# State products of the fourth and fifth chunk moved ahead of the layer products in a decay-attention and gated-MLP kernel

## Chip, cores and metric

One core of a Trainium2 chip runs the whole program in one launch. The metric is the device time of that core in microseconds: the median of three runs.

## What is computed

Decay attention over 2 batches, 8 heads, 768 positions and 64 columns a head, then two gated layers over the 1536 tokens of width 512. The attention part is computed in blocks, with a state of 64x64 per head that is carried from block to block:

```python
intra = np.einsum('bhic,bhjc->bhij', qb, kb) * Dmask[None]
intra = np.einsum('bhij,bhjd->bhid', intra, vb)
inter = np.einsum('bhid,bhde->bhie', qb * lam_pow[None], kv_state)
out[:, :, sl] = intra + inter
kb_dec = kb * rev_pow[None]
kv_state = lam_block[None, :, None, None] * kv_state + np.einsum('bhsd,bhse->bhde', kb_dec, vb)
...
a = x @ w_a
b = x @ w_b
return (a * b @ w_out).astype(np.float32)
...
h = np.maximum(np.maximum(x @ w1, x @ w2), x @ w3)
return (h @ w_out).astype(np.float32)
```

## The kernel before

The kernel takes the 768 positions in 6 chunks of 128, and each chunk for both batches at once (`pair(m)` gives the two indices n of chunk m, counted from 0, so the fourth and fifth chunk are m = 3 and m = 4). For a chunk TensorE does four kinds of small products: `scores(n)` (queries with keys, in 64x64 pieces of the array, closed by two small matmuls on zeros per quarter, L508), `earlier(n)` (queries with the state, 64x64, L575; called state products below), `within(n)` (masked scores with values, 128x64, L588; called masked products) and `update(n)` (keys with values, 128x64, L601).

Other engines work in between. `masked(n)` on VectorE multiplies the scores with the decay table (L521, two banks for each n, four instructions a chunk). `queries(n)` and `keys(n)` on GpSimd scale queries and keys (L548, L553). `carry(m)` on VectorE folds the update into the state `held`, which lies in the tile `stt`, in four quarters of two heads (L617). `taken(n)` on ScalarE copies the results out of PSUM.

Into these chunks the first layer is mixed. `layer1` is a generator: each `next(layer1)` puts one step of 12 matmuls of 384 columns into TensorE's stream (`plain_group`, L753), in which weights and inputs stand as a high and a low part, so that there are three products for each. After the chunks, the layers go on in a scheme with seven products of sums of blocks, which need sums such as S1, S2, S3 and S4 of the inputs (tile `x0s` for the first three chunks, `x1s` for the others) and T1 to T4 of the weights (tile `wd` for weight 1, `w` for weight 2). Each operand is split in two: a copy on ScalarE gives the high part (`hi`, `x0S`), a subtraction on VectorE or GpSimd the low part (`lo`, `x0S` again).

These sums and splits are tasks of a planner, `Pace`. It runs while the program is written, keeps an estimated time for each engine, and puts a task's next instruction into the program as soon as the engine is free by its estimate. An instruction marked `EITHER` goes to VectorE or GpSimd, whichever would end first by the estimate. A task stops at a `gate` until `pace.open` names it. So a change in the order of TensorE's work changes also which engine gets which sum and in which order. Within one engine the order is then fixed: each engine works through its own stream and waits at its head.

Of the kernel before, what the change touches and what calls it, by code (L numbers as in the profile page):

```python
# [169 lines left out]
def decay_attention_gated_mlps(ctx: ExitStack, tc: tile.TileContext, qkv: bass.AP, lam: bass.AP, wup: bass.AP, wdown: bass.AP, out: bass.AP):  # L170
# [7 lines left out]
    pace = Pace()  # L178

    def slot(name, dt=F32):  # L180
        return sp.tile([128, 1536], dt, tag="s", name=name)
# [7 lines left out]
    def rd(t):  # L189
        return t.bitcast(F32)  # L190

    def tt(e, o, a, b, op):
        (nc.vector if e == "DVE" else nc.gpsimd).tensor_tensor(out=o, in0=a, in1=b, op=op)  # L193

    def copy(o, a):
        nc.scalar.activation(out=o, in_=a, func=AF.Copy)  # L196
# [44 lines left out]
    def converted(m, width, roomy=False):  # L241

        load_to(m)
        double = raw.pop(m)[:, 0:width]
        yield ("ACT",), width + 60, "S"
        if width > WB:
            near = wp.tile([128, width], F32, tag="s", bufs=1, name=f"ws{m}")
            scaled(double, near)  # L250
            yield ("ACT",), width + 60, "S"
        t = slot(f"wd{m}") if roomy else hp.tile([128, 1792], F32, tag="h", name=f"w{m}")
        w = t[:, 0:width]
        below(double, w)
        if width == WB:
            near = t[:, WB:2 * WB]
            yield ("ACT",), width + 60, "S"
            scaled(double, near)
        if m not in BYDVE:
            yield ("ACT",), width + 330, "S"  # L260
            sign(double, w)
        if m > 1:
            load_to(m + 2)
        yield ("DVE",), width, "S"
        joined(near, w)
        if m in BYDVE:
            yield ("DVE",), width, "S"
            signed(near, w)
        return t
# [36 lines left out]
    def up_pair(m, i):  # L306

        o = wop[m] = {}
        if m > 0:
            yield "gate", ("done", m - 1)  # L310
        yield "gate", ("conv", m)
        plain = i < NPLAIN
        t = yield from converted(m, 1024, plain)
        if not plain:
            yield from block_sums(t)
        yield "gate", ("split", m)
        hi, lo = (slot(f"{x}{m}", F32R) if plain else hp.tile([128, 1792], F32R, tag="h", name=f"{x}{m}") for x in ("hi", "lo"))
        for s in (slice(0, 1024), slice(1024, 1792))[0:1 if plain else 2]:
            n = s.stop - s.start
            yield ("ACT",), n, "S"  # L320
            copy(hi[:, s], t[:, s])
            e = yield EITHER, n, "S"
            tt(e, lo[:, s], t[:, s], rd(hi[:, s]), ALU.subtract)
            for x, place in PLACE.items():
                if s.start <= place.start < s.stop:
                    o["B12" if plain and x == "T2" else x] = (hi[:, place], lo[:, place])
        pace.open(("done", m))
        if plain:
            yield "gate", ("late", m)
            last = slot(f"hl{m}", F32R)  # L330
            t6 = t.rearrange("p (a n) -> p a n", a=6)
            e = yield EITHER, 512, "S"
            tt(e, t6[:, 4:6], t6[:, 0:1].to_broadcast([128, 2, 256]), t6[:, 1:4:2], ALU.subtract)
            e = yield EITHER, 256, "S"
            tt(e, t6[:, 0], t6[:, 3], t6[:, 4], ALU.subtract)
            e = yield EITHER, 256, "S"
            tt(e, t6[:, 1], t6[:, 2], t6[:, 0], ALU.subtract)
            for s, names in ((slice(1024, 1536), ("T1", "T3")), (slice(256, 512), ("T4",)), (slice(0, 256), ("T2",))):
                n = s.stop - s.start
                h, l = (last[:, x:x + 256] for x in (0, 256)) if names[0] == "T4" else (hi[:, s], lo[:, s])  # L340
                yield ("ACT",), n, "S"
                copy(h, t[:, s])
                e = yield EITHER, n, "S"
                tt(e, l, t[:, s], rd(h), ALU.subtract)
                for k, x in enumerate(names):
                    o[x] = h[:, 256 * k:256 * k + 256], l[:, 256 * k:256 * k + 256]

    def block_sums(t):

        t7 = t.rearrange("p (a n) -> p a n", a=7)  # L350
        e = yield EITHER, 512, "S"
        tt(e, t7[:, 4:6], t7[:, 0:1].to_broadcast([128, 2, 256]), t7[:, 1:4:2], ALU.subtract)
        e = yield EITHER, 256, "S"
        tt(e, t7[:, 0], t7[:, 3], t7[:, 4], ALU.subtract)
        e = yield EITHER, 256, "S"
        tt(e, t7[:, 6], t7[:, 2], t7[:, 0], ALU.subtract)
# [47 lines left out]
    def open_to(what, m):  # L404
        if m < len(items):
            items_to(m)
            pace.open((what, m))
# [53 lines left out]
    def rows(i):  # L461
        return slice(64 * i, 64 * i + 64)

    def pair(m):
        return 2 * m, 2 * m + 1
# [90 lines left out]
    def place(n, h):  # L556
        w = h // 2 % 2
        banks, o = ob[n]
        return banks[h // 4][rows(h % 2), o + 128 * w:o + 128 * w + 128]
# [8 lines left out]
    def earlier(n):  # L568

        q = aq[n][:, 1024:1536]  # L570
        for w in range(2):
            for i in range(2):
                for x in range(2):
                    a = 2 * w + x
                    nc.tensor.matmul(  # L575
                        place(n, 4 * i + a), held[rows(i), n % 2, a], q[rows(i), 128 * a:128 * a + 128],
                        start=ob[n][1] == 0 and w == 0, stop=False, skip_group_check=True)
        pace.pe(0.5, max(at["qs", n], at["st"]))
# [401 lines left out]
    with tc.manual_schedule():  # L980
# [71 lines left out]
        def layer1_steps():  # L1052
            for i, j in ((0, 0), (1, 0), (0, 1)):
                if j == 0:
                    ga[i] = slot(f"g{i}")
                yield from plain_group(i, j)
                if (i, j) == (NPLAIN - 1, 0):
                    pace.open(("x0", "S3"))
                    pace.open(("x1", "sums"))
                if j == 1:  # L1060
                    finished1(0, Group("", i, j, None, None))
                    open_to("split", NPLAIN + 1)
            groups = [Group(f"u{i}_{j}", i, j, xo.get, gated) for i, j in plan]
            for i, _ in enumerate(in_slots(groups, each1, finished1)):
                if 7 * len(groups) - i == 3:
                    next(then)
                elif 7 * len(groups) - i == 5:
                    pace.need(gtasks[0, 0][0])
                yield
# [13 lines left out]
        yo = {}  # L1083
        then = down1(at1)
        layer1 = layer1_steps()

        def steps(task, n, e=None):
# [105 lines left out]
        for m in range(3, NC):  # L1193
            last = m == NC - 1
            if m == 4:
                load_to(NPLAIN)
                for i in range(2):
                    for n in pair(5):
                        load(n, i)
                load_to(NPLAIN + 1)  # L1200
                open_to("conv", NPLAIN)
                pace.open(("late", 1))
                open_to("split", NPLAIN)
            for n in pair(m):
                queries(n)
            if not last:
                for n in pair(m):
                    keys(n)
            for n in pair(m):
                scores(n)  # L1210
                masked(n)
            for _ in range(1 if last else 2):
                next(layer1)
            results(m, last)
            for n in pair(m):
                earlier(n)
            for n in pair(m):
                within(n)
            if last:
                for n in pair(m):  # L1220
                    for i in range(2):
                        taken(n, xa, part=i)
                        if n % 2 == i == 0:
                            operands(1)
                        x = f"A{n % 2 + 1}{i + 1}"
                        pace.open(("x1", x))
                        steps(xo[1].tasks[x], 2)
            else:
                for n in pair(m):
                    taken(n, xa)  # L1230
            if m == 3:
                pace.open(("x0", "sums"))
            if not last:
                for n in pair(m):
                    update(n)
                carry(m)
            else:
                next(layer1)
# [175 lines left out]
```

## Time and profile before

| | us |
|---|---|
| median of 3 runs | 500.21 (499.57 to 500.47) |
| profiled execution | 499.4 |
| its span, first to last instruction | 497.6 |
| TensorE busy (matmuls) | 493.3 (99%) |
| VectorE busy | 343.5 (69%) |
| ScalarE busy | 295.5 (59%) |
| GpSimd busy | 60.3 (12%) |

Busy times are of one profiled execution; the span lies 1.8 us under that execution's own time. The page calls TensorE's matmuls PE, VectorE DVE, ScalarE ACT and GpSimd POOL. A timeline row gives the start from the beginning of the span, the duration from the first start to the last end of the merged instructions, the engine, the line, what is written and read, the shape and the count. Square brackets name the idle time ahead of it and what ended it. Matmuls are pipelined, so rows on PE overlap by some tenths of a microsecond, and the distance between starts is what counts. Rows on the other engines overlap by 0.07 to 0.1.

### The profile page before, as it was taken

To read this page: it belongs to the slowest core of one execution; us is meant where nothing else is said; L and a number is where in the kernel's file an instruction comes from. 1 tells how busy PE (TensorE), PEld (TensorE's weight loads), DVE (VectorE), ACT (ScalarE), POOL (GpSimd) and SP (SyncE) were. 2 spreads that over 40 slices of the span, in tenths; PEclk is the share of its full clock that TensorE was granted. 3 is DMA by queue.
4 is the path that set the end of the run, shared out by engine and by line. 5 is a ranking of instruction groups with operands and counts; after the bars stand their busy time and mean duration, and the time that the engine had idled before them with its cause. 6 is when DMAs were issued, how large, how long until landed. Compare 5 with 4: busy or idle time off the path is not lost.

```text
span 497.6 us, 8202 instructions
## 1 busy us (share of the span) xinstructions
PE 493.3 (99%) x3351; PEld 465.3 (94%) x3351; DVE 343.5 (69%) x536; ACT 295.5 (59%) x464; POOL 60.3 (12%) x58
## 2 busy tenths in 40 slices
PE   9999999999999999999999999999999999999997
PEld 6999999999999999998888888999999999998897
DVE  6779886667657656577364189667867885787962
ACT  3867675654465654679572566545666455576561
POOL 4885201101111110120000000000000000000000
PEclk9999999999999999999999999999999999999999
DMA  8996002222222101315231022002202211120023
GB/s 301 414 413 231 1 0 86 84 86 86 86 86 85 60 8 61 126 65 189 87 95 76 0 84 86 0 1 85 86 1 84 86 63 65 63 65 0 22 107 126
DMA packets 10597, 46.66 MB, mean 94 GB/s; under 512 B 1216, under 2 KB 1472, under 8 KB 8000
## 3 DMA queue, kind: packets, MB, share of 16 engines
q1 hardware_dynamic: 10512, 46.14, 25.2%
q8 instruction: 26, 0.43, 0.4%
q14 instruction: 11, 0.09, 0.1%
q10 hardware_dynamic: 48, 0.00, 0.0%
HBM read 42.99 MB, written 3.15 MB: 93 GB/s over the span
## 4 chain that ended last, share of the span: by engine, by line
PE 99%; POOL 0%; ACT 0%; DVE 0%; issue 0%; POOLq 0%
PE yp L851 20%; PE zu L731 18%; PE zv L731 15%; PE bu L731 9%; PE bv L731 8%; PE p L753 5%; PE out L905 5%; PE xu L731 4%; PE xv L731 4%; PE zo L954 3%; PE o L588 2%; PE bo L954 1%; PE s L496 1%; PE o L575 1%; PE k L601 1%; PE s L503 1%
## 5 line engine op out<-in xcount | busy, mean ns | idle before, releaser
L193 DVE TENSOR_TENSOR lo<-w,hi 128x1024 fp32r<-128x1024 f32 (+2 forms) x39 | 42.5, 1091 | 11.6 <-ACT hi L196 11.4
L196 ACT ACTIVATE hi<-w 128x1024 fp32r<-128x1024 f32 (+2 forms) x40 | 37.4, 935 | 11.5 <-DVE w L193 4.9
L851 PE MATMUL yp<-gh,dh 128*128 128x512 f32 x108 | 42.0, 389 | 0.0
L851 PE MATMUL yp<-gl,dh 128*128 128x512 f32 x108 | 42.0, 389 | 0.0
L851 PE MATMUL yp<-gh,dl 128*128 128x512 f32 x108 | 42.0, 389 | 0.0
L783 POOL TENSOR_TENSOR g<-z1u,z6u 128x384 f32<-128x384 f32 x21 | 22.6, 1076 | 147.6 <-DVE z6u L765 147.6
L193 DVE TENSOR_TENSOR gl<-g,gh 128x512 fp32r<-128x512 f32 x36 | 25.2, 719 | 20.7 <-ACT gh L196 20.7
L239 DVE SCALAR_TENSOR_TENSOR w<-ws,w 128x1024 int32<-128x1024 int32 (+1 forms) x21 | 30.4, 1445 | 8.9 <-ACT w L228 6.8
L228 ACT ACTIVATE w<-wr 128x1024 f16<-128x1024 f32 (+2 forms) x26 | 33.1, 1273 | 0.2
L193 DVE TENSOR_TENSOR w<-w 128x256 f32<-128x256 f32 (+1 forms) x57 | 30.6, 538 | 1.3
L223 ACT ACTIVATE w<-wr 128x1024 int32<-128x1024 uint16 (+2 forms) x26 | 27.5, 1057 | 2.4 <-DVE lo L193 2.0
L765 DVE TENSOR_TENSOR z6u<-bu,z6u 128x384 f32<-128x384 f32 x21 | 11.7, 555 | 23.7 <-PE bu L731 23.7
L196 ACT ACTIVATE z6u<-zu 128x384 f32<-128x384 f32 x21 | 10.2, 486 | 27.4 <-PE zu L731 27.4
L196 ACT ACTIVATE gh<-g 128x512 fp32r<-128x512 f32 x36 | 21.4, 622 | 7.5 <-PE yp L851 7.5
L231 ACT ACTIVATE ws<-wr 128x1024 f32<-128x1024 f32 (+1 forms) x22 | 24.2, 1098 | 0.8 <-DMA wr<-wup_dram 0.8
L196 ACT ACTIVATE z7u<-zu 128x384 f32<-128x384 f32 x21 | 10.3, 492 | 23.5 <-PE zu L731 23.4
L851 PEld LDWEIGHTS yp<-gh,dh 128*128 128x128 f32 x108 | 20.3, 188 | 4.2
L851 PEld LDWEIGHTS yp<-gl,dh 128*128 128x128 f32 x108 | 20.3, 188 | 4.2
L851 PEld LDWEIGHTS yp<-gh,dl 128*128 128x128 f32 x108 | 20.3, 188 | 4.1
L731 PE MATMUL bu<-x1S,hi 128*128 128x384 f32 x88 | 22.3, 334 | 0.0
L731 PE MATMUL zu<-x1S,hi 128*128 128x384 f32 x88 | 22.3, 334 | 0.0
L731 PE MATMUL zu<-x1A,hi 128*128 128x384 f32 x84 | 21.3, 334 | 0.0
(260 smaller groups left out, 1448.2 us busy)
## 6 DMA issues: line engine op xcount, KB each, us to landing
wr<-wup_dram SPq DMA_DIRECT2D x20, 1024.0 KB, 4.7
wr<-wdown_dram SPq DMA_DIRECT2D x12, 768.0 KB, 4.3
aq<-qkv_dram SPq DMA_DIRECT2D x12, 512.0 KB, 7.8
av<-qkv_dram SPq DMA_DIRECT2D x6, 512.0 KB, 9.0
out_dram<-ob SPq DMA_DIRECT2D x11, 256.0 KB, 2.0
av<-qkv_dram SPq DMA_DIRECT2D x8, 256.0 KB, 8.3
wr<-wup_dram SPq DMA_DIRECT2D x2, 512.0 KB, 8.9
out_dram<-ob SPq DMA_DIRECT2D x2, 128.0 KB, 1.8
```

The lines of the kernel that those rows point to most:

```text
L193: (nc.vector if e == "DVE" else nc.gpsimd).tensor_tensor(out=o, in0=a, in1=b, op=op)
L196: nc.scalar.activation(out=o, in_=a, func=AF.Copy)
L223: nc.scalar.activation(out=w.bitcast(I32), in_=halves[:, :, 1], func=AF.Copy, scale=2.0 ** -13, bias=2.0 ** -14 - 0.5)
L228: nc.scalar.activation(out=o[:, :, 1], in_=high(double), func=AF.Copy, scale=2.0 ** -112)
L231: nc.scalar.activation(out=near, in_=high(double), func=AF.Copy, scale=2.0 ** -112)
L239: nc.vector.scalar_tensor_tensor(out=w, in0=near, scalar=3, in1=w, op0=ALU.logical_shift_left, op1=ALU.bitwise_or)
L731: nc.tensor.matmul(ps, w, x, start=p in FIRST and i == 0, stop=i == len(todo) - 1, skip_group_check=p not in FIRST)
L753: nc.tensor.matmul(ps, w, x, start=m == 0, stop=m == 11)
L783: nc.gpsimd.tensor_tensor(out=ga[g.n][:, tokens(g.j, 0)], in0=g.z[1], in1=g.z[6], op=ALU.mult)
L851: nc.tensor.matmul(ps[e], w[:, cols], g, start=k == 0 and m == 0, stop=k == K1 - 1 and m == 2)
L905: nc.tensor.matmul(ps, a[:, o:o + 128], w[:, s], start=k == 0 and n == 0, stop=k == K2 - 1 and n == 2)
L954: nc.tensor.matmul(ps, x[:, 128 * r:128 * r + 128], w, start=p in FIRST and n == 0, stop=n == 8, skip_group_check=p not in FIRST)
```

## The change

In the fourth and fifth chunk the two layer steps stood between scores and state products. They now stand between state products and masked products. The sixth chunk keeps its order. Besides, the last split of weight 1 (its block T2) gets a gate of its own, which opens with the second plain group of the first layer. The diff:

```diff
@@ -337,6 +337,8 @@
             tt(e, t6[:, 1], t6[:, 2], t6[:, 0], ALU.subtract)
             for s, names in ((slice(1024, 1536), ("T1", "T3")), (slice(256, 512), ("T4",)), (slice(0, 256), ("T2",))):
                 n = s.stop - s.start
+                if names[0] == "T2":
+                    yield "gate", ("plain", m)
                 h, l = (last[:, x:x + 256] for x in (0, 256)) if names[0] == "T4" else (hi[:, s], lo[:, s])
                 yield ("ACT",), n, "S"
                 copy(h, t[:, s])
@@ -1055,6 +1057,7 @@
                     ga[i] = slot(f"g{i}")
                 yield from plain_group(i, j)
                 if (i, j) == (NPLAIN - 1, 0):
+                    pace.open(("plain", i))
                     pace.open(("x0", "S3"))
                     pace.open(("x1", "sums"))
                 if j == 1:
@@ -1209,11 +1212,14 @@
             for n in pair(m):
                 scores(n)
                 masked(n)
-            for _ in range(1 if last else 2):
+            if last:
                 next(layer1)
             results(m, last)
             for n in pair(m):
                 earlier(n)
+            if not last:
+                for _ in range(2):
+                    next(layer1)
             for n in pair(m):
                 within(n)
             if last:
```

TensorE in the fifth chunk before, from the last matmul of its scores (p is a bank of layer products, o a bank of the attention's results, am the masked scores):

```order
L508 MATMUL s_1_697<-stt 64x2x64
L753 MATMUL p_726<-xh_201,hi_584 128x384
...
L753 MATMUL p_745<-xl_202,hi_584 128x384
L575 MATMUL o_0_764<-aq_426,stt 64x128 x2
...
L588 MATMUL o_0_764<-am_693,av_430 64x128 x2
```

The same place now:

```order
L510 MATMUL s_1_699<-stt 64x2x64
L577 MATMUL o_0_726<-aq_426,stt 64x128 x2
...
L755 MATMUL p_752<-xh_201,hi_588 128x384
...
L755 MATMUL p_775<-xl_202,hi_588 128x384
L590 MATMUL o_0_726<-am_695,av_430 64x128 x2
```

The 16 state products, which read `stt`, now follow the scores at once; the 24 layer products stand behind them. The fourth chunk reads the same.

VectorE from the split of weight 1 in the fourth chunk to the first mask of the fifth, before (g is the gated product of the first layer):

```order
L760 TENSOR_TENSOR g_445<-p_569,z_474 128x384
L193 TENSOR_TENSOR lo_585<-wd_566,hi_584 128x1024
L193 TENSOR_TENSOR x0s_444<-x_207 128x768
L617 SCALAR_TENSOR_TENSOR stt<-stt,tables,k_629 128x2x64 x4
L521 TENSOR_TENSOR am_693<-s_0_669,tables 128x512
```

and now:

```order
L762 TENSOR_TENSOR g_445<-p_573,z_459 128x384
L193 TENSOR_TENSOR lo_589<-wd_571,hi_588 128x1024
L762 TENSOR_TENSOR g_445<-p_591,z_474 128x384
L193 TENSOR_TENSOR x0s_444<-x_207 128x768
L193 TENSOR_TENSOR x0s_444<-x0s_444,x_200 128x768
L619 SCALAR_TENSOR_TENSOR stt<-stt,tables,k_629 128x2x64 x4
L523 TENSOR_TENSOR am_695<-s_0_671,tables 128x512
```

One of the two gating products and the sum S2 (`x0s` from `x0s` and `x`) now stand between the split and the state.

GpSimd from the scaled keys of the fifth chunk on, before:

```order
L553 TENSOR_TENSOR av_432<-av_432,tables 128x512
L193 TENSOR_TENSOR x0s_444<-x0s_444,x_200 128x768
L193 TENSOR_TENSOR wd_566<-wd_566 128x512
L548 TENSOR_TENSOR aq_654<-aq_654,tables 128x512
L548 TENSOR_TENSOR aq_656<-aq_656,tables 128x512
L193 TENSOR_TENSOR lo_784<-w_718,hi_783 128x768
L193 TENSOR_TENSOR x0s_444<-x_200,x0s_444 128x768
```

and now:

```order
L555 TENSOR_TENSOR av_432<-av_432,tables 128x512
L193 TENSOR_TENSOR wd_571<-wd_571 128x512
L193 TENSOR_TENSOR wd_571<-wd_571 128x256 x2
L550 TENSOR_TENSOR aq_656<-aq_656,tables 128x512
L550 TENSOR_TENSOR aq_658<-aq_658,tables 128x512
L193 TENSOR_TENSOR lo_589<-wd_571,hi_588 128x512
```

GpSimd gave the sums S2 and S4 and a split of 768 columns of weight 2 to VectorE, and took two sums of 256 and a split of 512 of weight 1 from it.

VectorE in the fifth chunk, from the join of weight 2 (L239) to the state, before:

```order
L239 SCALAR_TENSOR_TENSOR w_718<-ws_691,w_718 128x1024
L193 TENSOR_TENSOR w_718<-w_718 128x512
L193 TENSOR_TENSOR w_718<-w_718 128x256
L760 TENSOR_TENSOR g_725<-p_745,z_743 128x384
...
L193 TENSOR_TENSOR x0S_639<-x0s_444,x0S_639 128x768
L193 TENSOR_TENSOR lo_784<-w_718,hi_783 128x1024
L193 TENSOR_TENSOR x0S_721<-x0s_444,x0S_721 128x768
L617 SCALAR_TENSOR_TENSOR stt<-stt,tables,k_808 128x2x64 x4
```

and now:

```order
L239 SCALAR_TENSOR_TENSOR w_720<-ws_693,w_720 128x1024
L193 TENSOR_TENSOR w_720<-w_720 128x512
L193 TENSOR_TENSOR w_720<-w_720 128x256 x2
L193 TENSOR_TENSOR x0S_639<-x0s_444,x0S_639 128x768
L193 TENSOR_TENSOR lo_769<-w_720,hi_768 128x1024
L762 TENSOR_TENSOR g_751<-p_775,z_773 128x384
L193 TENSOR_TENSOR x0S_649<-x0s_444,x0S_649 128x768
L193 TENSOR_TENSOR lo_769<-w_720,hi_768 128x768
L193 TENSOR_TENSOR x0s_444<-x_200,x0s_444 128x768
L619 SCALAR_TENSOR_TENSOR stt<-stt,tables,k_813 128x2x64 x4
```

A split of 768 and the sum S4 joined the row ahead of the state that the sixth chunk reads.

## Rows read from the trace of the kernel before

**Rows 1.** The page, busy time, share of the span and instructions by engine.
```profile
PE 493.3 (99%) x3351; PEld 465.3 (94%) x3351; DVE 343.5 (69%) x536; ACT 295.5 (59%) x464; POOL 60.3 (12%) x58
```

**Rows 2.** Busy times by stretch; PEclk is TensorE's granted clock.
```profile
core 0: us, PE busy (x) PEld busy (x) DVE busy (x) ACT busy (x) POOL busy (x), PEclk, DMA share, GB/s
27.80:64.82 37.02, 37.02 (x596) 35.13 (x593) 33.56 (x52) 23.81 (x39) 18.04 (x12) 1.00 0.47 184
64.82:490.00 425.18, 425.18 (x2333) 403.76 (x2333) 288.92 (x441) 254.40 (x382) 22.59 (x21) 1.00 0.19 66
```

**Rows 3.** TensorE's timeline, fourth to sixth chunk: start, duration, instruction.
```profile
29.41 0.44 PE L753 MATMUL p<-xh,hi 128*128 128x384 f32 x1
...
33.51 0.34 PE L753 MATMUL p<-xl,hi 128*128 128x384 f32 x1
33.78 1.10 PE L575 MATMUL o<-aq,stt 64*64 64x128 f32 x32
34.81 1.97 PE L588 MATMUL o<-am,av 128*64 128x128 f32 x32
36.61 1.10 PE L601 MATMUL k<-av 128*64 128x64 f32 x32
...
39.25 0.44 PE L753 MATMUL p<-xh,hi 128*128 128x384 f32 x1
...
49.09 0.44 PE L753 MATMUL p<-xh,hi 128*128 128x384 f32 x1
...
51.38 1.10 PE L575 MATMUL o<-aq,stt 64*64 64x128 f32 x32
```

**Rows 4.** VectorE's timeline in the same chunks.
```profile
27.92 1.12 DVE L617 SCALAR_TENSOR_TENSOR stt<-stt,tables,k 128x128 f32<-128x128 f32 x4 [0.28 <-PE k L601]
...
35.43 1.78 DVE L193 TENSOR_TENSOR lo<-wd,hi 128x1024 fp32r<-128x1024 f32 x1 [0.76 <-POOL av L553]
37.14 0.94 DVE L193 TENSOR_TENSOR x0s<-x 128x768 f32<-128x768 f32 x1
38.01 1.11 DVE L617 SCALAR_TENSOR_TENSOR stt<-stt,tables,k 128x128 f32<-128x128 f32 x4
...
41.44 2.26 DVE L239 SCALAR_TENSOR_TENSOR w<-ws,w 128x1024 int32<-128x1024 int32 x1
43.73 1.65 DVE L193 TENSOR_TENSOR w<-w 128x512 f32<-128x512 f32 x1
45.41 0.42 DVE L193 TENSOR_TENSOR w<-w 128x256 f32<-128x256 f32 x1
45.75 0.55 DVE L760 TENSOR_TENSOR g<-p,z 128x384 f32<-128x384 f32 x1
...
47.42 1.22 DVE L193 TENSOR_TENSOR lo<-w,hi 128x1024 fp32r<-128x1024 f32 x1
...
50.46 2.47 DVE L521 TENSOR_TENSOR am<-s,tables 128x512 f32<-128x512 f32 x4
```

**Rows 5.** GpSimd's timeline in the same chunks.
```profile
24.10 2.99 POOL L548 TENSOR_TENSOR aq<-aq,tables 128x512 f32<-128x512 f32 x2
...
33.06 3.07 POOL L553 TENSOR_TENSOR av<-av,tables 128x512 f32<-128x512 f32 x2
38.25 1.85 POOL L193 TENSOR_TENSOR x0s<-x0s,x 128x768 f32<-128x768 f32 x1 [2.12 <-DVE x0s L193]
40.05 1.32 POOL L193 TENSOR_TENSOR wd<-wd 128x512 f32<-128x512 f32 x1
41.31 3.52 POOL L548 TENSOR_TENSOR aq<-aq,tables 128x512 f32<-128x512 f32 x2
```

**Rows 6.** ScalarE's timeline in the fifth chunk.
```profile
39.98 1.40 ACT L228 ACTIVATE w<-wr 128x1024 f16<-128x1024 f32 x1
...
42.05 0.85 ACT L196 ACTIVATE x0S<-x0s 128x768 fp32r<-128x768 f32 x1
...
45.93 1.06 ACT L196 ACTIVATE hi<-w 128x1024 fp32r<-128x1024 f32 x1 [0.69 <-DVE w L193]
```

## Prediction

> **What bounds the kernel now.** I read the page first. TensorE is busy for 493.3 us, 99% of the span [rows 1]. The busy times by stretch then show where the rest lies: from 27.80 to 490 us TensorE is busy in all of both stretches, at a granted clock of 1.00 [rows 2]. So the end is set by TensorE's own instruction stream: what lengthens or shortens that stream, or makes it wait, moves the end by the same amount, and no later slack gives it back. The question is then only what the change does to TensorE's stream and which waits it puts into it. For this I read TensorE's timeline from the fourth to the sixth chunk [rows 3], where one stage follows another with no gap, and the timelines of the engines that feed it: VectorE [rows 4], GpSimd [rows 5] and ScalarE [rows 6].
>
> The fourth chunk's stream is: scores, then from 29.41 two steps of layer products (24 matmuls, 4.37 us), from 33.78 the state products, from 34.81 the masked products, from 36.61 update and scores of the fifth chunk, whose layer products start at 39.25 [rows 3]. The state products need the state as `carry` of the chunk before has left it. VectorE writes that in four quarters, 38.01 to 39.12 [rows 4], just as the scores end. Today it matters to nobody: 4.37 us of layer products stand between. That cover is what the change takes away.
>
> **Part 1, fewer changes of array shape.** Scores and state products both use 64x64 pieces of the array, layer products all of it, masked products and update 128x64. Before, the shape changes three times from scores to masked products, after it twice. One change costs about 0.1: the last step from a layer product to a state product takes 33.78 - 33.51 = 0.27 against (33.51 - 29.41) / 23 = 0.18 for a step within the layer products [rows 3]. The change from 64x64 to 128x64 has no row that stands apart; 0.1 to 0.2 bounds it by its neighbours. I take 0.15 a chunk, for two chunks **-0.30** (-0.2 to -0.4).
>
> **Part 2, the fourth chunk's state products.** They would start near 29.3. The state is ready at 27.92 + 1.12 = 29.04 [rows 4], the queries that GpSimd scales at 24.10 + 2.99 = 27.09 [rows 5], and VectorE's and GpSimd's order is unchanged up to there. Price 0; the margin is 0.2.
>
> **Part 3, the fifth chunk's state products wait.** Now the state must be ready at 39.25 - 0.3 = 38.95 or so, and VectorE's order has changed too. After its split `lo` it does the gating product, the sum S1 and then the sum S2, which was GpSimd's; only then the state. GpSimd in turn does three sums of weight 1 (512, 256, 256 columns) at that moment.
>
> These meet at a shared resource. While GpSimd runs, VectorE's instructions with both inputs in SBUF stand still, and the reverse; the one that waits goes next. GpSimd's two scalings of queries start at 41.31, and the first, of 512 columns as the sum at 40.05 that took 1.32, is over at about 42.6; VectorE's bitwise join, asked for at 41.44, takes 2.26 and ends at 43.70, 1.1 after that; GpSimd's second ends at 44.83, 1.13 later; VectorE's sum of 512, asked for at 43.73, takes 1.65 and ends at 45.38, 0.55 later [rows 4, 5]. Freed after a wait, a GpSimd instruction takes some 0.16 less than its free duration (1.13 for 1.3). VectorE's split `lo` of 1024 starts at 35.43, GpSimd ends at 33.06 + 3.07 = 36.13, `lo` ends at 37.21: 1.08 instead of the 1.22 at 47.42, 0.14 less [rows 4, 5]. Masks and state updates, which read PSUM, aren't held: GpSimd's sum of 768 took 1.85 beside them [rows 5].
>
> The sum from the end of `lo`, 37.21, which nothing in the change moves:
> - GpSimd's sum of 512, waiting since 36.13: 1.32 - 0.16 = 1.16 [rows 5], to 38.37. The gating product, which reads PSUM, passes meanwhile.
> - VectorE's S1: 0.94 - 0.14 = 0.80 [rows 4], to 39.17.
> - GpSimd's first 256: an estimate from 1.32 for 512 and 1.85 for 768 is 0.79, less 0.16: 0.63, to 39.80. S2 depends on S1 and asks too late to keep its turn.
> - S2: 0.80, to 40.60.
> - The state: its fourth quarter ends 1.04 after the sum ahead of it (38.01 + 1.11 = 39.12 against 37.14 + 0.94 = 38.08 [rows 4]): 41.64; its first, a quarter of that after it, at 40.86.
> - A signal costs 0.1 (VectorE ends at 45.83, ScalarE starts at 45.93 [rows 4, 6]). The fourth quarter is read first by the sixth of 16 state products: 41.74. The other 11 of 16, of 1.03 in all (33.78 to 34.81 [rows 3]), take 0.71: the layer products start at 42.45.
>
> Without a wait they would start at 39.25 + 1.03 - 0.30 = 39.98. So TensorE waits **2.5 us**. The lower bound is that GpSimd takes no turn in between: then `lo` 37.21, gating product 0.47 more, two sums of 0.87 each (the next starts 0.07 before the end of one), the state's fourth quarter 1.04, so 40.46, signal and the 11 products: 41.27, a wait of 1.3. I take the upper value, since all four turns seen in the rows were kept.
>
> **Part 4, the sixth chunk.** Its code keeps its order, but VectorE reaches it late. TensorE: 42.45 + 4.37 + 1.80 (34.81 to 36.61) + 2.64 (36.61 to 39.25) + 2.29 (49.09 to 51.38) [rows 3] puts its state products at 53.55 and its masked products at 54.58. VectorE: the state ends at 41.64, the four masks take 2.47 [rows 4], to 44.04. GpSimd has its second 256 to 41.23, two scaled queries of 1.30 to 43.83, then a split of 512 that was VectorE's; ScalarE's copy for it comes at the latest at 41.38 + 3 x 0.85 = 43.93 [rows 6]. So the split runs to about 45.1, and VectorE's join, to which it is a neighbour whoever is first, ends at 45.1 + 1.08 = 46.18. Then come the sums of weight 2 (0.69, which is 0.55 + 0.14, and twice 0.42), a split of 768 (0.94 as the sum of that size), the split of 1024 (1.22), the gating product (0.55), another split of 768 and, both taken over from GpSimd, a third one and the sum S4 at 0.94 each, and the state (1.04), each starting some 0.07 before the end of the one ahead: 53.85; masks to 56.25 [rows 4]. Before, the masks ended at 50.46 + 2.47 = 52.93 and the masked products began at 51.38 + 1.03 = 52.41 without a wait.
>
> The state's fourth quarter, at 53.95, is wanted at 53.87: 0.1. The second of the four masks (55.15 with its signal) is wanted 0.22 into the masked products, at 54.90: 0.25. The fourth (56.35) is wanted at 56.05: 0.3. Together **0.65**; the lower bound is 0, if VectorE is 1.1 us earlier, the upper 1.7, the price if one more GpSimd turn falls in. I take 0.65, the value of the rows.
>
> The moved DMA issues cost nothing: the transfer of the sixth chunk's queries waits for the fourth chunk's state products, which come 4.4 us sooner. The later split of T2 costs nothing: its 256 columns are two short instructions (0.42 on VectorE [rows 4]), and the layer products that use them stand over 100 matmuls of 0.18 us behind the sixth chunk.
>
> **Sum.** -0.30 + 2.5 + 0.65 = +2.85 us. The profiled execution took 499.4 (span 497.6) and would take 502.25; the median before, 500.21, lies 0.8 above it, so the forecast is 500.21 + 2.85 = **503.1**.
>
> **Rivals.**
> 1. *GpSimd doesn't take turns between the sums* (its instruction starts too late or loses). Then the wait is 1.3, VectorE reaches the sixth chunk 1.2 sooner and TensorE too; with 0 to 0.65 there it gives 500.21 - 0.3 + 1.3 = 501.2 to 501.9. Against it: [rows 4, 5] show a turn in every meeting. Chance 0.12.
> 2. *No wait, the shape change alone counts* (the other side): the place is the start of the fifth chunk's state products, the price -0.30, the point from which it decides is a state ready by 38.95. 500.21 - 0.3 = 499.9. For it: today's state is ready at 39.12, only 0.2 late. Against it: S2 alone, 0.87, now stands ahead of it on VectorE. Chance 0.05.
> 3. *The clock falls in the wait.* TensorE would stand still from 39.2 to 40.9. In the trace of before the granted clock is at its upper level, 2.4 GHz, all the way, and between 27.80 and 490 us there is no gap in TensorE's stream at all [rows 2], so no row shows what a gap of 1.7 does. If the clock fell to 1.2 GHz, the 4.37 us of layer products behind it would take twice that: 503.1 + 4.4 = 507.5. Chance 0.05. [...]
>
> **How the numbers follow.** Forecast 0.78, rivals 0.12, 0.05, 0.05. A comparison of this kernel can tell about 0.2% from no change, 1.0 us. Slower by more: the forecast, the clock and half of rival 1, 0.88. Within: the other half and most of rival 2, 0.10. Faster: 0.02. The forecast's own spread is part 3 at 1.9 to 2.6, part 4 at 0 to 1.7 and the medians' 0.4: 501.6 to 504.8. With rival 1 the range is 501.0 to 504.8; 1 in 10 is left out on the sides.
>
> **What would show it.** TensorE's timeline would show a gap ahead of the fifth chunk's state products, ended by VectorE's state, some 1.7 us long and then a state stage of over 1.5 instead of 1.03; VectorE's two sums between 37.6 and 40.7 with durations over 0.94 each (1.5 and 1.4 with their waits); a second, smaller gap in the sixth chunk's masked products, ended by VectorE's masks; and the fourth chunk's state products straight behind its scores with no gap. It is wrong if the gap is missing or under 1 us, if the granted clock drops below 1, or if the layer products after the sixth chunk show new idle time.

## The result, and the profile after

The changed kernel takes 502.89 us (median of 6 runs, 502.12 to 503.68) against 499.98 us for the kernel before on the same chip. The ratio is 1.0059, with a 95% interval of 1.0043 to 1.0074: slower by 2.9 us. The forecast was 503.1, on the same side and for the reason given. Its single terms do less well than the total suggests, and the single times hold something that the forecast had put at one in twenty.

The 14 times of the changed kernel in all runs lie in two groups: seven at 502.1 to 502.4 us, all with a mean granted clock of 1.00, and seven at 503.1 to 503.7 us, five of these with a mean clock of 0.997. Of the other two one is traced and started late (below); the last, 503.38 us at 0.999, has no trace. The first group shows the change by itself, so its profile (the run a_fourth below, 502.19 us, span 500.3) is read first.

The page of the changed kernel: busy time, share of the span and instructions by engine, to set beside [rows 1].

```profile
PE 494.2 (98%) x3351; PEld 465.7 (93%) x3351; DVE 343.8 (69%) x536; ACT 295.7 (59%) x464; POOL 58.4 (12%) x58
```

The engines are as busy as before. What grew is the time in which TensorE stands still. To see where, I cut both traces at the start of each chunk's update: fourth, fifth and sixth chunk, the last one to the first layer product behind it. Kernel before, busy times by stretch:

```profile
36.61:46.45 9.84, 9.84 (x197) 9.24 (x194) 9.77 (x15) 7.36 (x11) 6.58 (x4) 1.00 0.85 318
46.45:54.31 7.86, 7.86 (x185) 7.09 (x181) 7.23 (x14) 4.11 (x10) 4.10 (x2) 1.00 0.01 2
```

Changed kernel (a_fourth), the same view; columns as in [rows 2]:

```profile
26.78:36.51 9.73, 9.73 (x193) 9.24 (x194) 7.24 (x12) 6.49 (x10) 8.86 (x8) 1.00 1.00 411
36.51:48.69 12.18, 10.38 (x197) 9.60 (x195) 12.04 (x18) 8.53 (x13) 8.34 (x6) 1.00 0.66 257
48.69:57.10 8.41, 8.41 (x185) 7.31 (x181) 8.41 (x15) 4.11 (x10) 0.00 (x0) 1.00 0.01 2
57.10:490.00 432.90, 432.90 (x2371) 411.45 (x2370) 295.61 (x451) 259.51 (x391) 22.71 (x21) 1.00 0.18 65
```

The fourth chunk took 9.89 us before (from 26.72) and takes 9.73 now, the fifth goes from 9.84 to 12.17 (the row above has rounded ends), the sixth from 7.86 to 8.41. Behind it TensorE is busy all the way, as before. The whole loss, 2.33 + 0.55 - 0.16 = 2.72 us, lies in some 30 us. TensorE's timeline of the same run, to set beside [rows 3]:

```profile
29.36 1.05 PE L577 MATMUL o<-aq,stt 64*64 64x128 f32 x32
...
38.99 0.22 PE L510 MATMUL s<-stt 64*64 64x128 bf16 x2
41.03 1.56 PE L577 MATMUL o<-aq,stt 64*64 64x128 f32 x32 [1.80 <-DVE stt L619]
42.52 0.45 PE L755 MATMUL p<-xh,hi 128*128 128x384 f32 x1
...
46.89 1.97 PE L590 MATMUL o<-am,av 128*64 128x128 f32 x32
...
53.62 1.53 PE L577 MATMUL o<-aq,stt 64*64 64x128 f32 x32
55.08 2.09 PE L590 MATMUL o<-am,av 128*64 128x128 f32 x32
```

The fourth chunk's state products start straight behind the scores. The fifth chunk's stand idle for 1.80 us, ended by VectorE's state, and then take 42.52 - 41.03 = 1.49 us in place of 1.03, as the state arrives in quarters. VectorE and GpSimd at the same place, to set beside [rows 4, 5]:

```profile
35.47 1.79 DVE L193 TENSOR_TENSOR lo<-wd,hi 128x1024 fp32r<-128x1024 f32 x1 [0.76 <-POOL av L555]
37.19 0.54 DVE L762 TENSOR_TENSOR g<-p,z 128x384 f32<-128x384 f32 x1
37.65 1.56 DVE L193 TENSOR_TENSOR x0s<-x 128x768 f32<-128x768 f32 x1
39.25 1.37 DVE L193 TENSOR_TENSOR x0s<-x0s,x 128x768 f32<-128x768 f32 x1
40.55 1.11 DVE L619 SCALAR_TENSOR_TENSOR stt<-stt,tables,k 128x128 f32<-128x128 f32 x4
...
52.73 1.12 DVE L619 SCALAR_TENSOR_TENSOR stt<-stt,tables,k 128x128 f32<-128x128 f32 x4
53.76 2.48 DVE L523 TENSOR_TENSOR am<-s,tables 128x512 f32<-128x512 f32 x4
```

```profile
36.14 5.07 POOL L193 TENSOR_TENSOR wd<-wd 128x512 f32<-128x512 f32 x3
41.18 2.53 POOL L550 TENSOR_TENSOR aq<-aq,tables 128x512 f32<-128x512 f32 x2
```

S1 takes 1.56 us and S2 1.37, where the sum S1 took 0.94 in [rows 4], and beside them GpSimd's three sums run from 36.14 to 41.21. The state's fourth quarter ends at 40.55 + 1.11 = 41.66, behind the end of `lo` (35.47 + 1.79 = 37.26) by 4.40 us; the prediction had 41.64 - 37.21 = 4.43.

**The second group.** The profiled execution of the result itself took 503.67 us, at a granted clock of 1.00. Its trace differs ahead of all that the change moves: TensorE's masked products of the second chunk start late, and so does GpSimd's scaling of that chunk's keys. Changed kernel, first profile, TensorE and then GpSimd:

```profile
16.56 1.20 PE L590 MATMUL o<-am,av 128*64 128x128 f32 x18 [1.82 <-DVE w L239]
```

```profile
16.49 2.08 POOL L555 TENSOR_TENSOR av<-av,tables 128x512 f32<-128x512 f32 x2 [3.55 <-DMA av<-qkv_dram]
```

TensorE's wait is put down to VectorE, but GpSimd's row names what both need: the transfer of `av`, which landed late. In the other three profiles of the changed kernel this wait is missing, so it belongs to the execution. It makes the fourth chunk start 1.9 us later (28.67 against 26.78), and the whole run is 1.5 us longer: the fifth chunk takes 11.68 us there in place of 12.17, since VectorE and GpSimd, which make TensorE wait, had been held up less than TensorE (VectorE's `lo` starts 1.39 us later than in a_fourth, 36.86 against 35.47).

### The profile page after: what moved, and what is told of

Read it like the earlier page. It is cut to its first block, busy times and chain, and to the rows that moved or that the text cites. A ratio compares the mean times of both kernels' runs of the same rounds, so it can differ in the third digit from the quotient of the medians.

```text
span 501.8 us, 8197 instructions
## 1 busy us (share of the span) xinstructions
PE 494.2 (98%) x3351; PEld 465.7 (93%) x3351; DVE 343.8 (69%) x536; ACT 295.7 (59%) x464; POOL 58.4 (12%) x58
## 4 chain that ended last, share of the span: by engine, by line
PE 95%; DMA 2%; DVE 1%; SPq 0%; ACT 0%; issue 0%
PE yp L853 20%; PE zu L733 17%; PE zv L733 15%; PE bu L733 9%; PE bv L733 7%; PE p L755 5%; PE out L907 5%; PE xu L733 4%; PE xv L733 4%; PE zo L956 3%; DMA wr<-wup_dram 2%; PE o L590 2%; PE bo L956 1%; PE o L577 1%; PE xo L956 1%; PE s L505 1%
## 5 line engine op out<-in xcount | busy, mean ns | idle before, releaser
L239 DVE SCALAR_TENSOR_TENSOR w<-ws,w 128x1024 int32<-128x1024 int32 (+1 forms) x21 | 29.7, 1413 | 9.2 <-ACT w L228 6.8
L193 DVE TENSOR_TENSOR w<-w 128x256 f32<-128x256 f32 (+1 forms) x57 | 29.1, 511 | 1.3
```

The source lines that it names most:

```text
L239: nc.vector.scalar_tensor_tensor(out=w, in0=near, scalar=3, in1=w, op0=ALU.logical_shift_left, op1=ALU.bitwise_or)
```

## Experiments

Two theories stand against each other. **Theory:** VectorE delivers the state late because of what it now does ahead of it, in turns with GpSimd; TensorE pays wherever it first meets the late state. **Rival:** the layer step in front of the state products was the cover, and its loss alone is the price, whatever VectorE does.

The outcome of all kernels, read from their profiles in the same cut (distances of the starts, in us):

| kernel | 4th chunk | 5th | 6th | median, ratio to before (95%) |
|---|---|---|---|---|
| before | 9.89 | 9.84 | 7.86 | 499.6 to 500.0 |
| changed, first profile | 9.73 | 11.68 | 8.44 | 502.89, 1.0059 (1.0043 to 1.0074) |
| changed, a_fourth | 9.73 | 12.17 | 8.41 | 502.19, one run |
| changed, a_third | 9.73 | 13.68 | 7.86 | 503.59, one run |
| changed, a_again | 9.73 | 13.65 | 7.86 | 502.69, 1.0050 (1.0032 to 1.0068) |
| e9 | 9.73 | 9.97 | 7.86 | 499.70, 0.9994 (0.9984 to 1.0004) |
| e10 | 9.89 | 9.84 | 10.78 | 502.55, 1.0054 (1.0034 to 1.0074) |
| e3 | 9.73 | 10.63 | 9.12 | 502.01, 1.0042 (1.0028 to 1.0056) |
| e3b | 9.73 | 11.10 | 8.16 | 501.08, 1.0027 (1.0017 to 1.0038) |
| e2 | 9.73 | 9.68 | 12.39 | 504.03, 1.0089 (1.0075 to 1.0102) |
| e9b | 9.73 | 9.68 | 8.26 | 500.92, 1.0026 (1.0015 to 1.0036) |
| e5_only4 | 9.73 | 9.84 | 11.78 | 504.98, 1.0109 (1.0093 to 1.0125) |
| e6_only5 | 9.89 | 9.92 | 9.90 | 502.08, 1.0051 (1.0037 to 1.0064) |

**e9: TensorE's move without the planner's.** TensorE's stream is that of the changed kernel, while the planner is told of the state products where they stood before, and the gate of T2 is left out, so the orders of VectorE, GpSimd and ScalarE are those of the kernel before. The edit, against the changed kernel:

```diff
-                if names[0] == "T2":
-                    yield "gate", ("plain", m)
...
-    def earlier(n):
+    def earlier(n, told=True):
...
+        if told:
+            state_told(n)
+    def state_told(n):
         pace.pe(0.5, max(at["qs", n], at["st"]))
...
-                earlier(n)
+                earlier(n, last)
             if not last:
                 for _ in range(2):
                     next(layer1)
+                for n in pair(m):
+                    state_told(n)
```

> The move on TensorE alone: fourth and fifth chunk's state products stand directly behind the scores, as in the changed kernel, but VectorE, GpSimd and ScalarE keep the order of the kernel before, so S2 stays on GpSimd and S4 stays behind the masks. Theory (the wait is made by VectorE's later state, which the new order there makes): the fifth chunk's state products wait at most 0.3 us, the sixth chunk's nothing more than before, and the two saved shape changes stay: 499.7 to 500.3 us. Rival (the wait is made by the lost cover of the layer products in front of the state products, whoever makes the state): a wait of some 1 us or more remains, 500.7 us or more.

The time is 499.70, no change. TensorE's and VectorE's timelines in the fifth chunk:

```profile
39.26 1.34 PE L575 MATMUL o<-aq,stt 64*64 64x128 f32 x32
40.53 0.44 PE L757 MATMUL p<-xh,hi 128*128 128x384 f32 x1
```

```profile
37.68 0.95 DVE L193 TENSOR_TENSOR x0s<-x 128x768 f32<-128x768 f32 x1
38.55 1.12 DVE L621 SCALAR_TENSOR_TENSOR stt<-stt,tables,k 128x128 f32<-128x128 f32 x4
```

The cover is gone here as well, and there is no idle time: the state products start at 39.26 and take 1.27, 0.28 over the 0.99 of an unhindered stage, as the fourth quarter ends at 39.67. So the move on TensorE costs next to nothing by itself; the rival falls. No run takes T2's gate alone away; e6_only5 below has that gate, and S2 stays on GpSimd there, so the gate by itself does not move S2.

**e10: the planner's move without TensorE's.** The reverse: TensorE has its stream of before, the other engines the order of the changed kernel (`earlier` is split as in e9).

```diff
-            results(m, last)
-            for n in pair(m):
-                earlier(n)
             if not last:
+                for n in pair(m):
+                    state_told(n)
                 for _ in range(2):
                     next(layer1)
+            results(m, last)
+            for n in pair(m):
+                earlier(n, last)
```

> The other half: VectorE, GpSimd and ScalarE have the order of the changed kernel, TensorE has the order of the kernel before (layer products ahead of the state products in all chunks). Theory (VectorE is late by what it took over, and the lateness is paid wherever TensorE first meets it): nothing or little in the fifth chunk, where the layer products cover the wait again, but the sixth chunk's state products then wait for VectorE's state and masks: 2.3 to 2.8 us, 502.3 to 502.8 us. Rival (the lost cover is the cause): no wait, 500.0 to 500.5 us.

The fifth chunk takes 9.84 us as before, the sixth 10.78. What TensorE waited for, in us:

```profile
PE p L759 <- ACT x L196: 1.0, 1, 1.0
PE o L577 <- DVE stt L623: 0.8, 1, 0.8
```

The time is 502.55, all but the changed kernel's, though TensorE's stream is untouched. The loss belongs to the other engines' order, and with the cover in place it is paid one chunk later. Of the sixth chunk's 2.92 us more, 1.8 are these waits; most of the rest lies in the state products, which take 1.87 in place of 1.03 at the pace of the state's quarters. One part was not expected: 1.0 of the waiting comes through ScalarE. Its timeline:

```profile
47.83 1.79 ACT L196 ACTIVATE hi<-w 128x1024 fp32r<-128x1024 f32 x2 [1.35 <-DVE w L193]
49.52 1.19 ACT L196 ACTIVATE x<-o 128x256 f32<-128x256 f32 x4
```

The copies that empty the fifth chunk's banks, which begin at 46.89 in the trace of before, stand behind two high halves, and these wait for VectorE's sums. VectorE's lateness comes to TensorE by way of a third engine.

**e3: the turns.** GpSimd's three sums of weight 1 are left out; writes of zeros stand in their place.

```diff
-            tt(e, t6[:, 4:6], t6[:, 0:1].to_broadcast([128, 2, 256]), t6[:, 1:4:2], ALU.subtract)
+            nc.gpsimd.memset(t6[:, 4:6], 0.0)
...
-            tt(e, t6[:, 0], t6[:, 3], t6[:, 4], ALU.subtract)
+            nc.gpsimd.memset(t6[:, 0], 0.0)
...
-            tt(e, t6[:, 1], t6[:, 2], t6[:, 0], ALU.subtract)
+            for _ in range(10): nc.gpsimd.memset(t6[:, 1], 0.0)
```

> The changed kernel with GpSimd's three sums of the plain weight block (one of 512 columns, two of 256) left out: writes of zeros stand in their place, repeated so that GpSimd's next scaling starts about when it did, so the output is not the reference's. VectorE's order is the changed kernel's. Theory (VectorE's two sums S1 and S2 take 1.57 and 1.38 us because they take turns with GpSimd's sums): without these they take about 0.87 us each, the state comes 1.1 to 1.7 us earlier, the fifth chunk's wait shrinks by as much, and the time falls to 501.2 to 501.9 us. Rival (VectorE is late only because it has more to do, the turns do not matter): the sums keep 1.4 to 1.6 us and the time stays at 502.5 to 503.2 us.

The time missed the expectation: 502.01, its lower times at 501.8 to 502.0. VectorE's timeline, then GpSimd's:

```profile
39.16 0.95 DVE L193 TENSOR_TENSOR x0s<-x 128x768 f32<-128x768 f32 x1
40.14 0.96 DVE L193 TENSOR_TENSOR x0s<-x0s,x 128x768 f32<-128x768 f32 x1
...
46.35 1.67 DVE L193 TENSOR_TENSOR w<-w 128x512 f32<-128x512 f32 x1
```

```profile
39.09 3.63 POOL L337 MEMSET wd<- 128x256 f32 x10
...
45.29 2.18 POOL L193 TENSOR_TENSOR lo<-wd,hi 128x512 fp32r<-128x512 f32 x1
```

The sums are back at 0.95 and 0.96 beside GpSimd's writes: the turns did lengthen them, by 0.61 and 0.41. This profile, too, starts late (its fourth chunk at 28.81), so it is set beside the first profile of the changed kernel (28.67): the fifth chunk is 11.68 - 10.63 = 1.05 us shorter, about what those two lengths add up to. The sixth chunk is 0.7 longer (9.12 against 8.44). The Trainium skill, "SBUF — State Buffer", section "Who interferes with whom", says that a VectorE instruction with two SBUF inputs contends with a GpSimd instruction that reads SBUF and not with one that only writes it; these rows agree, 0.95 beside writes and 1.37 to 1.56 beside sums.

**e3b: where the gain went.** In e3 a low half of 512 on GpSimd (45.29, 2.18 us) met VectorE's sum of 512, 1.67 in place of 0.69. This run leaves that low half out as well.

```diff
-                tt(e, l, t[:, s], rd(h), ALU.subtract)
+                nc.gpsimd.memset(rd(l), 0.0) if n == 512 else tt(e, l, t[:, s], rd(h), ALU.subtract)
```

> The run without GpSimd's three sums of weight 1 once more, with GpSimd's next low half of 512 columns left out too (a write of zeros in its place). In the run before, the fifth chunk's wait fell by 1.06 us, as the theory of turns has it, but the time fell by only 0.3 us against the changed kernel's undisturbed times: this low half ran from 45.29 to 47.46 us beside a low half of 512 columns on VectorE, which took 1.67 us in place of 0.69, and the sixth chunk waited 0.7 us longer. Theory (the gain was given back by turns at a later place): without that low half VectorE's takes 0.7 us again, the sixth chunk's waits shrink to 0.6 us or less, and the median is 501.0 to 501.5 us. Rival (the fifth chunk's wait is not what the time hangs on): 502 us again.

The time is 501.08, in the range of the theory. VectorE's sum of 512, merged with two of 256 (the three took 1.61 in a_fourth too):

```profile
45.05 1.61 DVE L193 TENSOR_TENSOR w<-w 128x512 f32<-128x512 f32 x3
```

The fifth chunk is 12.17 - 11.10 = 1.07 us shorter than in a_fourth, and nothing is given back: the sixth takes 8.16. So 1.07 of the 2.5 us is the turns, shown at the place and in the time. The other 1.42 has about the size of S2 itself, 0.88 from start to start, and of the gating product, 0.47, which now stand ahead of the state as well; that split is worked out, and no run takes the gating product alone away.

**e2: the state ahead of the sums.** One gate is moved so that VectorE writes the fifth chunk's state before S1 and S2.

```diff
-            if m == 3:
-                pace.open(("x0", "sums"))
...
                 carry(m)
+                if m == 3:
+                    pace.open(("x0", "sums"))
```

> The changed kernel with one gate moved: the sums S1 and S2 are let go behind the call that writes the fifth chunk's state, so on VectorE the state stands ahead of both; the planner then also places a few later pieces elsewhere. Theory (the fifth chunk waits because S1 and S2 stand ahead of the state on VectorE, so what S1 and S2 take is the price): the fifth chunk's wait goes from about 2 us to at most 0.3 us; the two sums still have to be made ahead of the sixth chunk's state, so a wait of 0.5 to 1.5 us with that chunk's state products and masks stays: 500.3 to 501.5 us. Rival (TensorE needs the layer step in front of the state products, whatever VectorE does first): the fifth chunk still waits 1 us or more and the time is 502 us or more.

The first half came as the theory says: the fifth chunk takes 9.68, both shape changes saved and no wait. The second half did not; the time is 504.03. What TensorE waited for, VectorE's and GpSimd's timelines, and the busy times by stretch behind the wait:

```profile
PE o L577 <- DVE stt L619: 2.3, 1, 2.3
```

```profile
37.16 0.55 DVE L762 TENSOR_TENSOR g<-p,z 128x384 f32<-128x384 f32 x1
37.91 1.12 DVE L619 SCALAR_TENSOR_TENSOR stt<-stt,tables,k 128x128 f32<-128x128 f32 x4 [0.20 <-PE k L603]
...
49.71 1.22 DVE L193 TENSOR_TENSOR lo<-w,hi 128x1024 fp32r<-128x1024 f32 x1
50.85 2.57 DVE L193 TENSOR_TENSOR x0s<-x,x0s 128x768 f32<-128x768 f32 x1
```

```profile
50.19 2.42 POOL L193 TENSOR_TENSOR lo<-w,hi 128x768 fp32r<-128x768 f32 x1 [8.58 <-ACT hi L196]
```

```profile
53.82:58.83 5.01, 5.01 (x65) 4.40 (x65) 4.39 (x10) 2.42 (x5) 1.82 (x1) 0.66 0.00 0
```

The gating product still stands ahead of the state, and the state even waits 0.20 us for TensorE's update: without the sums the gating product alone makes no wait. The planner also put a low half of 768 on GpSimd. It asks at 50.19, waits for VectorE's `lo` until 50.93, runs to 52.61, and S4, straight ahead of the state, takes 2.57 in place of 0.95. The wait was moved to the sixth chunk and made longer by one turn, 1.6 us, and the granted clock in the chunk's products behind it is 0.66 in the mean. Beside its wait the sixth chunk loses 2.22 us here and 1.02 in e5_only4 below, where the clock stays at 1.00, so about 1.2 us is an estimate of what the clock took; all four runs of e2 have a mean clock of 0.996.

**e9b: the same gate in e9.** The edit is that of e2, made to e9.

> The move on TensorE alone, as in the run before with that edit, and the same gate moved: the fifth chunk's state stands ahead of S1 on VectorE. Theory: the 0.28 us that the fifth chunk's state products still lost to the pace of the state's quarters go, and both shape changes are saved, 0.3 us in all: 499.3 to 499.7 us. Rival: S1 and what follows it on VectorE are late for the sixth chunk instead, 499.8 to 500.5 us.

A miss: 500.92. The fourth and fifth chunk save 0.16 each, as meant, but the sixth takes 0.40 more and the layer products behind it 1.2 more. VectorE's timeline and what TensorE waited for behind the chunks:

```profile
46.29 2.04 DVE L193 TENSOR_TENSOR w<-w 128x256 f32<-128x256 f32 x2
```

```profile
PE p L757 <- DVE x1A L193: 0.4, 1, 0.4
```

Here the planner had put a low half of 768 on GpSimd; two short sums on VectorE take 2.04 us beside it, twice 0.42 alone. No version beats the kernel before.

**e5_only4 and e6_only5: one chunk each.** The order of state products and layer steps is changed for m = 3 alone, or for m = 4 alone.

```diff
-            if last:
-                next(layer1)
+            first_layer = m != 3
+            if first_layer:
+                for _ in range(1 if last else 2):
+                    next(layer1)
...
-            if not last:
+            if not first_layer:
```

> Only the fourth chunk's state products stand straight behind the scores; the fifth chunk has its layer products first, as before. S2 still moves to VectorE, since the planner decides that in the fourth chunk. Theory (lateness of VectorE, paid where TensorE first meets it): no wait in the fifth chunk, where the layer step covers it, and 1 to 1.5 us in the sixth, by its state products and masks: 500.9 to 501.9 us. Rival (each moved chunk costs its own lost cover): the fourth chunk's move is free and the time is 499.8 to 500.2 us.

> Only the fifth chunk's state products stand straight behind the scores; S2 stays on GpSimd, while a low half of 768 columns and S4 now stand ahead of the sixth chunk's state on VectorE. Theory: the fifth chunk waits at most 0.3 us, the sixth 1 to 1.6 us for state and masks, since VectorE has 1.9 us more ahead of them: 500.7 to 501.4 us. Rival (the lost cover in the fifth chunk is the cause): 1.5 us or more in the fifth chunk and nothing in the sixth, 501.5 us or more.

In both the place is as the theory says, the fifth chunk without a wait (9.84, and 9.92, where the state products take 1.21 in place of 0.99) and the loss in the sixth. The size is not: 504.98 and 502.08. e5_only4, waits, then VectorE and GpSimd ahead of the state, and the busy times behind the wait:

```profile
PE o L577 <- DVE stt L619: 2.9, 1, 2.9
```

```profile
49.92 2.60 DVE L193 TENSOR_TENSOR x0S<-x0s,x0S 128x768 fp32r<-128x768 f32 x1
52.44 1.48 DVE L193 TENSOR_TENSOR lo<-w,hi 128x768 fp32r<-128x768 f32 x1
```

```profile
48.95 2.76 POOL L193 TENSOR_TENSOR x0s<-x,x0s 128x768 f32<-128x768 f32 x1 [6.45 <-DVE x0S L193]
51.66 2.84 POOL L193 TENSOR_TENSOR wd<-wd 128x256 f32<-128x256 f32 x2
```

```profile
54.33:58.21 3.88, 3.88 (x65) 3.12 (x65) 3.88 (x9) 1.48 (x3) 0.18 (x1) 1.00 0.00 0
```

In e5_only4 the planner gives S4 to GpSimd, and that is no time saved on VectorE: S4 and the two sums behind it run beside VectorE's queue and make two instructions take 2.60 and 1.48 in place of 0.95 each. The profiled run, 503.69 us, is the only one of five whose mean clock is 0.999; the other four have 0.993 to 0.996 and take 504.87 to 506.63, so part of the median, too, goes with a lower clock. In e6_only5 the sixth chunk loses 2.04, and 0.9 more is lost behind the chunks, where two waits of 0.3 us on VectorE are new; I had looked no further than the sixth chunk.

**a_again, a_third, a_fourth: the changed kernel again.**

> The changed kernel a second time. In its first trace the second chunk's masked products began 2.09 us behind its state products, where the kernel before has 0.20, ahead of all that the change moves. If that is a transfer that lands late in some executions, single times of this kernel lie about 1 us apart, and a profile without the late start shows a longer wait for the state in the fifth chunk (2.5 us, as predicted, where the first trace has 2.0), since VectorE and GpSimd, not TensorE, set when the state is ready. If the late start belongs to the change, it stands in this profile too with the same 1.9 us. Median 502.1 to 503.7 either way.

> The changed kernel once more, for a profile without the late start of the first one and, if it comes so, without the lower clock of the second one: then the fifth chunk costs 2.0 to 2.6 us more than before (wait and pace of the state's quarters together), the sixth 0.4 to 0.6 us, and the run is 502.1 to 502.4 us. If the granted clock falls behind the wait again, 503 to 503.6 us.

> The same once more: 502.1 to 502.4 us where the granted clock stays at 1.00, 503 to 503.6 us where it falls behind the wait in the fifth chunk.

None of the three has the late start. a_fourth came as expected: 2.33 more in the fifth chunk, 0.55 in the sixth, 502.19 us. The other two show the clock. a_third, busy times of the idle wait, the state products and the layer step behind it; then the same stretches of a_fourth (the third number from the right is the granted clock):

```profile
39.67:41.39 1.72, 0.00 (x1) 0.03 (x1) 1.72 (x3) 1.69 (x2) 1.64 (x2) 1.00 0.98 401
41.39:43.51 2.12, 2.12 (x33) 1.66 (x33) 2.12 (x6) 1.65 (x3) 2.12 (x3) 0.68 0.47 128
43.51:48.84 5.33, 5.33 (x27) 5.08 (x25) 5.23 (x7) 2.12 (x4) 1.81 (x2) 0.81 0.42 175
```

```profile
39.23:41.03 1.80, 0.00 (x0) 0.03 (x1) 1.78 (x3) 1.77 (x2) 1.72 (x2) 1.00 0.96 396
41.03:42.52 1.49, 1.49 (x32) 1.18 (x32) 1.49 (x5) 1.12 (x3) 1.49 (x3) 1.00 0.59 165
42.52:46.89 4.37, 4.37 (x27) 4.12 (x25) 4.30 (x6) 1.60 (x3) 2.49 (x2) 1.00 0.57 229
```

After an idle time of 1.72 us the clock fell towards its lower level, 1.2 GHz, in one execution (0.68 and 0.81 are means of stretches at both levels); after 1.80 us it stayed at the upper level, 2.4 GHz, in the other. It costs 0.63 in the state products and 0.96 in the layer step, but the sixth chunk then finds its state and masks ready and takes 7.86 in place of 8.41. The two chunks together are 21.54 against 20.58 us: 0.96 net.

## Why the prediction held, step by step

- **What bounds the kernel.** Right. Behind the sixth chunk the two traces run alike, and no slack gave back what was lost ahead of it.
- **Part 1, -0.30.** Right: 0.16 saved wherever a chunk's products were moved, 9.89 to 9.73 and, in e2 and e9b without a wait, 9.84 to 9.68.
- **Part 2, price 0.** Right: 29.36, straight behind the scores.
- **Part 3, 2.5.** Right in size and, to 0.04, in every step of its ladder. In the undisturbed profile the fifth chunk is 2.33 longer with 0.16 saved: 2.49. S1 ends 1.95 behind `lo` (predicted 1.96), S2 3.36 (3.39), the state 4.40 (4.43). e9 and e10 show that the loss is made by the other engines' order, e2 that the sums ahead of the state make the wait, e3 and e3b that the turns are in it.
- **Part 4, 0.65.** The size nearly held, 0.55, but not its split. I had put 0.1 on the state and 0.55 on the second and fourth mask; it is 55.08 - 53.62 - 1.03 = 0.43 in the state products and 0.12 in the masked ones. I had reckoned only when the fourth quarter is read. Of the 0.43, the trace puts 0.2 down to the first mask. State products do not read what a mask writes, so by the code this can only be a bank that held scores and comes free when the mask has read them; no run tests that. The state's end came out as forecast, 52.73 + 1.12 = 53.85, but the sum behind that figure has a slip: with 0.07 of overlap at every step it gives 53.65, and 53.85 needs the first two sums of weight 2 to start 0.03 behind the instruction ahead, as [rows 4] have it. By the step that the text gives, part 4 would have been 0.45.
- **The sum.** 2.85 predicted, 2.72 measured. For the profiled execution I had 502.25, and the undisturbed runs are at 502.1 to 502.4. The last step, 0.8 more since the median of before lay 0.8 above its profile, was wrong: the later comparisons have that median at 499.6 to 499.8. That the median came out at 502.89 after all is luck: it is due to the second group of times, which the forecast did not contain. Two smaller slips: the chance of a slower kernel adds up to 0.89, not 0.88, and the three terms of the spread, all low or all high, give 501.4 and 504.6, not 501.6 and 504.8.
- **Rival 1 and rival 2** fell. The turns were kept. Rival 2 shows only in a kernel without the planner's part: e9 has no wait, and of the 0.32 saved the pace of the state's quarters takes 0.28 back.
- **Rival 3, the clock, 0.05.** This chance was too low and its price too high. A lower clock shows in both traced runs with a mean clock of 0.997, and five of 14 runs have that mean. I priced it at the whole layer step at half speed, 4.4 us; the clock came back within that step (0.81), and 0.55 was given back in the sixth chunk, so it costs 1.0. With it one of the forecast's own signs of being wrong, a granted clock below 1, came true in some of the executions; the other two, a gap under 1 us and new idle time behind the sixth chunk, did not in a_fourth. The Trainium skill, "TensorE: Matmul & The Clock Gate", section "HAM oscillation — how this bites in real kernels", describes a kernel in which the wait for data between two groups of matmuls makes the gate halve the clock for the next group; the waits there are longer than those here. In this case the clock fell behind 1.93, 1.72 and 2.31 us (a_again, a_third, e2), and a_fourth shows the same kernel without it.

## What to carry to other kernels

Where a planner writes the order of all engines from an estimate of one, a move on the bound engine is two changes, and the second can be the larger: compare the queues of the helpers before pricing the move, and run each half alone. Here a vector instruction with both inputs in SBUF that fell beside a GpSimd instruction took up to nearly that instruction's length on top of its own (2.57 us in place of 0.95, behind a low half of 768 that takes GpSimd 1.82 alone), so ahead of a value for which the bound engine waits, work handed to GpSimd wasn't work saved. When the helper has little slack, removing a wait at one stage only moves it: look two stages on before counting the gain.

## What was not expected of the hardware

- The granted clock fell behind an idle time of 1.72 us in one execution and not behind 1.80 in another of the same kernel, nor behind the longest wait seen, 2.90 us, in the profile of e5_only4, whose four other runs have mean clocks of 0.993 to 0.996. What decides it stays open. In the kernel before, TensorE has no such gap, and all its 20 runs beside the first four experiments show a clock of 0.999 or 1.000.
- The late transfer of the second chunk's `av` delays a run by 1.9 us at its start. Four of those 20 runs of the kernel before lie at 501.4 to 501.7, the others at 499.5 to 500.1; without their traces, that this is the same transfer stays open.
- A wait behind another engine takes up part of such a delay: 1.9 us at the start came out as 1.5 us at the end.
